# One slot of a chunked recurrence with a feed-forward stage: its small products gathered in three runs

## The chip, the cores and the metric

The kernel runs on one core of a Trainium2 chip. The metric is the device time in microseconds of one execution. TensorE (PE) multiplies matrices, VectorE (DVE), ScalarE (ACT) and GpSimd (POOL) work element by element, and SyncE (SP) issues transfers. [...]

## The reference

For each of 4 x 8 heads a state of 40x40 is carried over 768 positions. Its readings are joined over the heads, and each of the 3072 rows of 320 goes through a feed-forward stage with a gated softmax and a normalization.

```python
for t in range(S):
    y[:, :, t] = np.einsum('bhd,bhde->bhe', rt, state)
    Sa = np.einsum('bhde,bhe->bhd', state, at)
    state_decay = state * wt[:, :, None, :] - np.einsum('bhd,bhe->bhde', Sa, bt)
    state = state_decay + np.einsum('bhd,bhe->bhde', vt, kt)
...
h = x @ w_in
e = np.exp(h - h_max)
sm = e / (np.sum(e, axis=-1, keepdims=True) + 1e-09)
solu = h * sm
ln = (solu - mu) / np.sqrt(var + 1e-06) * g_ln
return (ln @ w_out).astype(np.float32)
```

## The kernel before

The 768 positions are cut into 12 chunks of 64. Two batches with 8 heads each make one item, so 24 items i follow each other, in turn from the two pairs of batches; item i uses the state that item i - 2 left. Within a chunk the recurrence becomes a triangular system, which is solved with the inverse of two 32x32 diagonal blocks and a coupling between them.

The main loop has one turn, called a slot, for each i from -1 to 27. A slot works on several items at once: it answers and reads item i, prepares scores and couplings of item i + 1, keys of items i + 5 to i + 8, and the feed-forward stage of items that were read two to four slots before (m = i - 1, with m - 3, m - 2 and m - 1). TensorE, GpSimd, VectorE and SyncE execute in the order in which the program names the steps; only ScalarE's order is found by the scheduler. So the order of the calls in the loop is the order of the queues.

The steps, by the names that the profile shows:

- `front` transposes a (pa) and b (pb); VectorE forms aT, ScalarE copies bT. `decay` makes the cumulative decays (lw, pcum, ei, inv), `decay_turned` turns them (pei, ex), `scaled` multiplies b and k on GpSimd (kb).
- `norm` multiplies aT and bT (pnt); VectorE masks the product (nt), and a transfer brings it to memory. `begin_inverse` reads it back in blocks (blk) and puts a generator into a list; `some(n)` takes n steps from that list, each of two VectorE operations (prod, uu; L415 and L417). An inverse of 30 steps serves two items; its result goes out (uu_dram) and `bring` fetches it into tu and uh. `narrow` does the same steps, and in the first slots it also converts parts of the weights.
- `flip` transposes a part of tu on VectorE (L442). `couple` multiplies nt with it (py), ScalarE scales the result (wy, L454). `close` multiplies wy with uh (pz), and the copy completes tu.
- `attend_kv` and `attend_rs` transpose k, v, r (pk, pv, pr) and the state (pst). `scores` forms two products (ps); VectorE masks them into psi and lv.
- `carried` and `driven` form the right-hand side (px) out of the state and out of psi; ScalarE copies it to x0. `solved` multiplies with the inverse (pu; nuT, lu). `answered` multiplies with rT (pl), masked into lu.
- `read` forms answers and new state (pyo) in two halves: own (row half and column half of the array equal) and not own. `leave` scales them on VectorE (x, tot) and GpSimd (st) and sends x by transfers to xT; `left` sends the rest of it.
- `hidden` is the first feed-forward product (h): for k-tiles 0 and 1 with 128 rows, for k-tile 2 two products of 64 rows. `exped` takes the maximum (nmax, VectorE) and the exponential (e, ScalarE), `weighed` multiplies e by h, `spreadof` takes the statistics (bs, mv, c; all VectorE), `folded` transposes e (plnT), `output` is the second product (po) in two halves of four.

PSUM has three pools: two buffers of the shape of `banks` (pnt, py, pz, px, ps, pu, pl, pyo in turn), two of `bank` (all transposes, pcum, po), and one h. A product that takes a buffer waits until the readers of the tile two allocations back are done.

The small products are 64x64 (or 40x64): a helper orders 16 of them so that neighbours use different quarters of the array. Where two groups add into the same result from different rows of the array, `fence` puts a drain of TensorE between them. Before, there are two: between `carried` and `driven`, and between the halves of `read`.

Of the kernel before, what the change touches and what calls it, by code (L numbers as in the profile page):

```python
# [17 lines left out]
P = 128  # L18
# [3 lines left out]
GRP = 2  # L22
# [26 lines left out]
def kernel(  # L49
# [204 lines left out]
        nc.tensor.matmul(o, lhsT=lhsT, rhs=rhs, start=start, stop=stop, skip_group_check=True)  # L254


    def fence():
        nc.tensor.drain()

# [19 lines left out]
    def ok(i):  # L279
        return 0 <= i < N  # L280


    def load_keys(i, names, queue=nc.sync):
        if not ok(i):
            return
        for n, ap in (("w", w), ("b", b), ("a", a), ("k", k)):
            if n in names:
                x = a_t[i % 4] if n == "a" else two.tile([P, H, D], FP32, tag="raw_" + n, name="raw_" + n,
                                                             bufs=3)
                st[i]["raw_" + n] = x  # L290
                load(x, ap, i, queue)
# [18 lines left out]
    def decay(i):  # L310
        if not ok(i):
            return
        d = st[i]
        lw = two.tile([P, DM], FP32, tag="lw", name="lw", bufs=1)
        nc.scalar.activation(out=lw, in_=d["raw_w"].rearrange("p h d -> p (h d)"), func=AF.Ln)
        t = (bank("pcum") if i > 5 else ps2.tile([P, DFF], FP32, tag="h", name="h"))[:, 0:DM]
        nc.tensor.matmul(t, lhsT=c_("cum"), rhs=lw, start=True, stop=True)
        nc.scalar.activation(out=ei_t[0][:, :, 0:D], in_=heads(t), func=AF.Exp)
        inv = d["inv"] = two.tile([P, DM], FP32, tag="inv", name="inv", bufs=4)
        nc.scalar.activation(out=inv, in_=t, func=AF.Exp, scale=-1.0)  # L320
# [10 lines left out]
    def turned(name, x):  # L331
        t = bank("p" + name)
        for j in range(4):
            nc.tensor.transpose(out=t[0:W2, j * P:(j + 1) * P],  # L334
                                in_=x[:, 2 * j:2 * j + 2].rearrange("p a b -> p (a b)")[:, 0:W2], identity=ident)
        return t[0:W2].rearrange("p (j b t) -> p b j t", j=4, b=2)
# [4 lines left out]
    def kept(name, t, bufs=1):  # L341
        o = tokens(name, bufs)
        nc.scalar.copy(out=o[0:W2], in_=t)
        return o
# [7 lines left out]
    def front(i):  # L352
        if not ok(i):
            return
        d = st[i]
        t = turned("a", d["raw_a"])
        aT = d["aT"] = tokens("aT", AHEAD)
        nc.vector.tensor_tensor(out=aT[0:W2], in0=t, in1=d["ex"][0:W2, :, :, 0:C], op=ALU.mult)
        d["bT"] = kept("bT", turned("b", d["kb"][:, H:]))

    def masked(dst, t):
# [112 lines left out]
        d["kT"] = kept("kT", turned("k", d["kb"]))  # L474
        d["vT"] = kept("vT", turned("v", v_t[0]))

    def attend_rs(i):
        if not ok(i):
            return
        d = st[i]  # L480
        bp, ci = where_(i)
        d["rT"] = kept("rT", turned("r", r_t[0]), 2)
        if ci:
            t = bank("pst")
            for x in range(4):
                nc.tensor.transpose(out=t[0:W2, x * P:(x + 1) * P],
                                    in_=st_t[bp][:, 2 * x:2 * x + 2].rearrange("p a b -> p (a b)")[:, 0:W2], identity=ident)
            d["s"] = two.tile([P, 4, P], FP32, tag="s", name="s")
            nc.scalar.copy(out=d["s"][0:W2], in_=t[0:W2].rearrange("p (x t) -> p x t", x=4))

    def scores(i):
# [33 lines left out]
    def driven(i):  # L525
        if not ok(i):
            return
        d = st[i]
        if d["opened"]:
            fence()  # L530
        for u in in_turn(lambda p, q, g, h: (p, p ^ h)):
            p, q, g, h = u
            j = 2 * q + g
            mm(d["px"][half(p ^ h), h, j * D:j * D + D], d["psi"][half(p), h, j],
               d["lv"][half(p), head(u), C:W2], start=(h, p ^ h) not in d["opened"])
            d["opened"].add((h, p ^ h))
        nc.scalar.copy(out=x0[:, :, :, 0:D], in_=d["px"][:, :, 0:4 * D].rearrange("p h (j d) -> p h j d", j=4))
# [31 lines left out]
    def read(i, own):  # L569
        if not ok(i):  # L570
            return
        d = st[i]
        bp, ci = where_(i)
        if own:
            d["po"] = banks("pyo")
            d["opened"] = set()
            if ci:
                for u in in_turn(lambda p, q, g, h: (q, h)):
                    p, q, g, h = u
                    at = (2 * p + g) * W2  # L580
                    mm(d["po"][half(h), q, at:at + C], d["s"][rows(q), 2 * p + g, h * C:h * C + C], valued(d["rT"], u),
                       start=(q, h) not in d["opened"], stop=False)
                    d["opened"].add((q, h))
        else:
            fence()
        for g in range(2):
            for j in range(2):
                for u in in_turn(lambda p, q, g, h: (p, h), [u for u in units if (u[0] == u[1]) == own and u[2] == g]):
                    p, q, g_, h = u
                    at = (2 * p + g) * W2  # L590
                    mm(d["po"][half(h), q, at:at + W2], d["kb"][half(p), j * H + head(u)],
                       d["lu" if j else "lv"][half(p), head(u), 0:W2], start=(q, h) not in d["opened"], stop=j == 1)
                    d["opened"].add((q, h))
# [44 lines left out]
    def hidden(i, some):  # L638

        if not ok(i):  # L640
            return
        d = st[i]
        for kt, x in some:
            if (kt, x) == (0, 0):
                d["h"] = ps2.tile([P, DFF], FP32, tag="h", name="h")
            part = slice(0, P) if kt < 2 else half(x)
            mm(d["h"][:, 512 * x:512 * x + 512], d["xT"][part, kt], w_in[part, 2 * kt + (x if kt < 2 else 0)],
               start=kt == 0, stop=kt == NK - 1)

    def exped(i):  # L650
        if not ok(i):
# [61 lines left out]
    def some(n):  # L713
        while steps and n:
            if next(steps[0], steps) is steps:
                steps.pop(0)
            else:
                n -= 1
# [18 lines left out]
    for i in range(4):  # L737
        scaled(i, "b")
        if i == 3:
            scaled(0, "k")  # L740
            scaled(1, "k")
        front(i)
        decay(i + 1)
        norm(i)
        decay_turned(i + 1)
        if i == 0:
            load_keys(2, "ba")
        if i == 1:
            load_keys(3, "w")
            begin_inverse(0)  # L750
            narrow(2)
            load_keys(3, "ba")
            load_keys(0, "k")
            load_keys(4, "w")
            some(8)
        if i == 2:
            load_values(0)
            load_keys(1, "k")
            some(8)
    load_keys(5, "w")  # L760
    load_keys(4, "ba")
    begin_inverse(1)
# [7 lines left out]
    decay(5)  # L770
    load_keys(6, "w")
    land(3, nc.sync)
    some(14)
    load_keys(5, "ba")
    load_values(1)
    bring(0)
# [2 lines left out]
    for n in (4, len(lands)):  # L779
        land(n, nc.sync)  # L780


    shares = {-1: (0, 6, 2, 6), 0: (0, 6, 4, 6), 1: (0, 6, 3, 6), 2: (0, 6, 3, 6), 3: (0, 6, 3, 6)}
    narrowed = {-1: (0, 1), 0: (1, 1), 1: (1, 2), 2: (1, 2), 3: (1, 1)}
    for i in range(-1, N + 3 + LAG):
        j, m = i + AHEAD, i - LAG
        pieces = shares.get(i, (3, 6, 0, 6))
        some_weights = narrowed.get(i, (0, 0))

        some(pieces[0])  # L790
        if i >= 1:
            bring(i + 1)
        if i >= 0:
            load_values(i + 2)
        carried(i)
        driven(i)
        front(j)
        hidden(m - 2, ((0, 1),))
        if i == 3 + LAG:
            centred(mean, 6)  # L800
        load_keys(j + 3, "w")
        load_keys(j + 2, "bak")
        narrow(some_weights[0], pieces[1])

        solved(i)
        attend_kv(i + 1)
        hidden(m - 2, ((1, 1),))
        norm(j)
        attend_rs(i + 1)
        hidden(m - 2, ((2, 0), (2, 1)))  # L810
        exped(m - 2)
        decay_turned(j + 1)
        scaled(j + 1)
        left(i - 1)

        answered(i)
        if i >= 0:
            flip(i + 1)
        weighed(m - 2)
        spreadof(m - 2)  # L820
        decay(j + 2)
        if i == 0:
            turn_g()
        if i == 2 + LAG:
            mean = mean_begun(6)
        output(m - 3, 0)
        if ok(j) and j % GRP == GRP - 1:
            begin_inverse(j // GRP)
        some(pieces[2])
        scores(i + 1)  # L830
        if i < 0:
            flip(i + 1)
        couple(i + 1)
        output(m - 3, 1)
        narrow(some_weights[1], pieces[3])

        close(i + 1)
        read(i, True)
        read(i, False)
        by_value(i + 2)  # L840
        leave(i)
        folded(m - 2)
        hidden(m - 1, ((0, 0), (1, 0)))


# [28 lines left out]
```

## Time and profile before

| | us |
|---|---|
| median of three runs | 640.13 |
| lowest, highest | 639.94, 641.92 |
| the profiled execution | 639.79 |
| its span, first to last instruction | 637.7 |

| stretch of the span | PE busy | DVE busy | clock granted to TensorE |
|---|---|---|---|
| 60 to 110 (first slots) | 35.68 of 50 | 43.81 | 0.70 |
| 110 to 170 | 51.68 of 60 | 53.79 | 0.85 |
| 333.9 to 356.4 (one slot) | 22.28 of 22.5 | 17.61 | 1.00 |
| 356.4 to 378.8 (the next) | 22.18 of 22.4 | 17.34 | 1.00 |

Busy is the time in which an engine executed something; the clock is the share of the full TensorE clock that was granted. In the timelines a line has start, duration, engine, line or operation, what was written and read, the shapes, and in brackets the idle time before and what ended it. [...] the duration of one overlaps the start of the next: step from start to start, or from end to end in the chain of waits.

### The profile page before, as it was taken

What the parts mean: (1) busy time and instruction counts of PE and PEld (TensorE: products, weight loads), DVE (VectorE), ACT (ScalarE), POOL (GpSimd) and SP (SyncE); (2) the same over time, 40 slices, a digit from 0 to 9 for tenths busy, and PEclk for the clock granted to TensorE, in tenths of its full rate; (3) what the DMA queues carried; (4) which work ended last, traced back from release to release, by engine and by line L of the source; (5) the groups of instructions that cost most, each with busy time, mean ns of one, the idle gap of its engine ahead of it and who ended that gap; (6) DMA issues with size and microseconds to landing.
All of it is one profiled execution on the core that took longest, in us unless ns stands there. A gap on an engine that the chain in (4) does not pass through costs nothing.

```text
span 637.7 us, 26729 instructions
## 1 busy us (share of the span) xinstructions
PE 567.5 (89%) x11451; PEld 399.6 (63%) x11451; DVE 461.9 (72%) x1286; ACT 245.3 (38%) x498; POOL 269.1 (42%) x444
## 2 busy tenths in 40 slices
PE   5245677988999999999999999999999999999995
PEld 3134555756577677667667767666776666766653
DVE  4678799999878778778878777787887796443431
ACT  3412545554334434433443443344243333332221
POOL 3334345574274444445543642743544642222200
PEclk9665676688999999999999999999999999999998
DMA  8939896474355535544554553654423422210000
GB/s 166 159 73 169 170 164 131 107 152 87 71 110 93 111 87 95 107 93 103 103 120 79 108 116 73 119 107 95 91 53 70 98 49 49 51 36 26 24 20 21
DMA packets 217868, 59.92 MB, mean 94 GB/s; under 512 B 203216, under 2 KB 213048, under 8 KB 217752
## 3 DMA queue, kind: packets, MB, share of 16 engines
q1 hardware_dynamic: 200984, 34.47, 31.7%
q0 software_dynamic: 11376, 19.25, 12.6%
q10 hardware_dynamic: 5392, 4.51, 2.5%
q8 instruction: 90, 1.47, 1.0%
q14 instruction: 26, 0.21, 0.1%
HBM read 40.10 MB, written 13.37 MB: 84 GB/s over the span
## 4 chain that ended last, share of the span: by engine, by line
PE 71%; DVE 13%; DMA 6%; issue 4%; ACT 2%; SPq 2%; POOL 1%; DVEq 0%; ACTq 0%; POOLq 0%
PE h L254 16%; PE po L703 14%; PE pyo L254 7%; PE px L254 4%; PE pu L254 3%; DVE uu L417 3%; PE plnT L692 3%; PE ps L254 3%; DVE prod L415 3%; PE pl L254 2%; PE pr L334 2%; PE pnt L254 2%; PE pk L334 2%; PE pa L334 2%; PE pz L254 2%
## 5 line engine op out<-in xcount | busy, mean ns | idle before, releaser
L254 PE MATMUL h<-w_in,xT 128*128 128x512 f32 (+1 forms) x288 | 121.6, 614 | 0.0
L415 DVE TENSOR_TENSOR prod<-blk,uu 128x30 f32<-128x30 f32 (+4 forms) x360 | 99.0, 275 | 24.0 <-DMA blk<-nt_dram 14.0
L703 PE MATMUL po<-w,lnT 128*128 128x320 f32 x384 | 113.5, 440 | 0.0
L417 DVE TENSOR_TENSOR uu<-uu,prod 128x30 f32<-128x30 f32 (+4 forms) x360 | 101.9, 283 | 12.4
L703 PEld LDWEIGHTS po<-w,lnT 128*128 128x128 f32 x384 | 70.5, 190 | 29.3 <-issue 2.3
L655 DVE TENSOR_REDUCE nmax<-h 128x1 f32<-128x1024 f32 x24 | 29.4, 1224 | 60.0 <-PE h L254 59.9
L388 POOL DMA_DIRECT2D nt_dram<-nt x20 | 18.3, 916 | 119.0 <-DVE nt L362 97.7
L254 PEld LDWEIGHTS h<-w_in,xT 128*128 128x128 f32 (+1 forms) x288 | 38.9, 190 | 21.9 <-issue 20.8
L623 POOL TENSOR_TENSOR st<-tot,ex 104x160 f32<-104x160 f32 x44 | 22.1, 520 | 70.4 <-DVE tot L619 68.2
L681 POOL TENSOR_TENSOR rs<-c,mhalf 128x1 f32<-128x1 f32 x24 | 13.4, 559 | 91.0 <-DVE c L680 89.6
L635 POOL DMA_DIRECT2D xT<-x x96 | 48.7, 512 | 0.0
L254 PE MATMUL pyo<-lv,kb 64*64 64x104 f32 x768 | 38.6, 274 | 6.0 <-DVE lv L362 3.3
L693 ACT COPY lnT<-plnT 128x512 f32<-128x512 f32 x48 | 26.1, 589 | 43.3 <-PE plnT L692 43.3
L399 POOL DMA_DIRECT2D blk<-nt_dram x42 | 33.3, 800 | 13.0 <-DMA nt_dram<-nt 12.7
L658 ACT ACTIVATE e<-h,nmax 128x1024 f32<-128x1024 f32 x24 | 26.8, 1115 | 28.6 <-DVE nmax L655 27.5
L254 PE MATMUL pyo<-lu,kb 64*64 64x104 f32 x768 | 37.2, 266 | 0.0
L664 DVE TENSOR_TENSOR e<-h,e 128x1024 f32<-128x1024 f32 x24 | 29.4, 1225 | 10.1 <-ACT e L658 10.1
L276 POOL DMA_DIRECT2D raw_r<-in_r_dram x48 | 34.9, 729 | 0.3 <-issue 0.3
L672 DVE BATCH_NORM_STATS2 bs<-e 128x6 f32<-128x512 f32 x48 | 30.9, 686 | 0.8
L707 ACT ACTIVATE osb<-po,rs 128x320 f32<-128x320 f32 x24 | 12.7, 528 | 48.5 <-PE po L703 29.6
L254 PEld LDWEIGHTS pnt<-aT,bT 40*64 40x64 f32 x768 | 14.6, 144 | 26.5 <-issue 25.0
L254 PEld LDWEIGHTS pyo<-lv,kb 64*64 64x64 f32 x768 | 23.9, 145 | 11.3 <-issue 7.7
(130 smaller groups left out, 1127.0 us busy)
## 6 DMA issues: line engine op xcount, KB each, us to landing
blk<-nt_dram POOLq DMA_DIRECT2D x42, 128.0 KB, 4.2
nt_dram<-nt POOLq DMA_DIRECT2D x20, 256.0 KB, 3.5
raw_w<-in_w_dram SPq DMA_DIRECT2D x48, 80.0 KB
a<-in_a_dram SPq DMA_DIRECT2D x48, 80.0 KB
raw_r<-in_r_dram POOLq DMA_DIRECT2D x48, 80.0 KB, 3.3
lv<-in_v_dram SPq DMA_DIRECT2D x48, 80.0 KB
out_dram<-osb ACTq DMA_DIRECT2D x24, 160.0 KB
raw_b<-in_b_dram SPq DMA_DIRECT2D x44, 80.0 KB
```

Source lines behind the costliest of these rows:

```text
L254: nc.tensor.matmul(o, lhsT=lhsT, rhs=rhs, start=start, stop=stop, skip_group_check=True)
L276: queue.dma_start(out=x[half(p), :, 0:D], in_=ap[2 * bp + p, :, ci * C:(ci + 1) * C, :].rearrange("h t d -> t h d"))
L334: nc.tensor.transpose(out=t[0:W2, j * P:(j + 1) * P], in_=x[:, 2 * j:2 * j + 2].rearrange("p a b -> p (a b)")[:, 0:W2], identity=ident)
L399: queue.dma_start(out=nb[home:home + Q], in_=blocks[n][:, Q * e:Q * e + Q, Q * e:Q * e + Q])
L415: nc.vector.tensor_tensor(out=t, in0=nb[:, j:j + 1, j + 1:Q].to_broadcast([P, n_c, m]), in1=u[:, 0:n_c, j:j + 1].to_broadcast([P, n_c, m]) ...
L417: nc.vector.tensor_tensor(out=u[:, 0:n_c, j + 1:Q], in0=u[:, 0:n_c, j + 1:Q], in1=t, op=ALU.subtract)
L635: nc.gpsimd.dma_start(out=xT[to:to + Q, 2], in_=x[at + P - 3 * D:at + D, 2])
L655: nc.vector.tensor_reduce(out=nmax, in_=d["h"], axis=AX.X, op=ALU.max, negate=True)
L658: nc.scalar.activation(out=e, in_=d["h"], func=AF.Exp, bias=nmax, accum_out=d["esum"])
L664: nc.vector.tensor_tensor(out=d["e"], in0=d["h"], in1=d["e"], op=ALU.mult)
L672: nc.vector.bn_stats(out=bs[:, x], in_=d["e"][:, x * 512:x * 512 + 512])
L703: nc.tensor.matmul(d["out"][:, 0:DM], lhsT=d["lnT"][:, f, :], rhs=w2[:, f, :], start=f == 0, stop=f == NF - 1)
```

## The change

The steps stay the same in what they compute; their order in the slot changes, and some are cut in two. `front` loses its b part to `front_b`; `attend_rs` becomes `attend_r` (the transpose of r) and `stated` (that of the state, with one buffer for s instead of two). `hidden` starts its accumulation with k-tile 2 and ends it with k-tile 1.

A slot then has the order: solved, scores of i + 1; stated, front, one h, front_b, decay_turned, one h, exped, decay, output's first half, weighed, spreadof; flip, couple, norm, answered; output's second half; close, the own half of read, carried of i + 1, the two 64-row products of h, one fence, the other half of read, driven of i + 1; then leave, folded, h, keys and values of i + 2, h, and r of i + 2. `carried` and `driven` are now done a slot earlier, for i + 1, and share the drain of `read`. The steps of the inverse are shared out as 3, 5, 3 and 4 instead of 3, 6, 0 and 6. On VectorE, flip thus stands behind weighed and spreadof of its slot. In the slots before the main loop, some steps of the inverse are moved, and keys, values and r of item 0 are prepared there.

```diff
+    def front_b(i):
+        if not ok(i):
+            return
+        d = st[i]
         d["bT"] = kept("bT", turned("b", d["kb"][:, H:]))
...
-    def attend_rs(i):
+    def attend_r(i):
+        if not ok(i):
+            return
+        st[i]["rT"] = kept("rT", turned("r", r_t[0]), 2)
+
+    def stated(i):
...
-            d["s"] = two.tile([P, 4, P], FP32, tag="s", name="s")
+            d["s"] = two.tile([P, 4, P], FP32, tag="s", name="s", bufs=1)
...
     def driven(i):
-        if d["opened"]:
-            fence()
...
     def read(i, own):
-        else:
-            fence()
...
     def hidden(i, some):
         for kt, x in some:
-            if (kt, x) == (0, 0):
+            if (kt, x) == (NK - 1, 0):
                 d["h"] = ps2.tile([P, DFF], FP32, tag="h", name="h")
...
-               start=kt == 0, stop=kt == NK - 1)
+               start=kt == NK - 1, stop=kt == NK - 2)
...
+        front_b(i)
         decay(i + 1)
+        some(4 * (i > 1))
         norm(i)
...
-            some(8)
+            some(4)
...
-    some(14)
+    some(10)
...
+    attend_kv(0)
+    attend_r(0)
...
     for i in range(-1, N + 3 + LAG):
         j, m = i + AHEAD, i - LAG
-        pieces = shares.get(i, (3, 6, 0, 6))
+        pieces = shares.get(i, (3, 5, 3, 4))
         some_weights = narrowed.get(i, (0, 0))
-
-        some(pieces[0])
         if i >= 1:
             bring(i + 1)
         if i >= 0:
             load_values(i + 2)
-        carried(i)
-        driven(i)
+        some(pieces[0])
+
+        solved(i)
+        scores(i + 1)
+        load_keys(j + 3, "w")
+        load_keys(j + 2, "bak")
+
+        stated(i)
         front(j)
         hidden(m - 2, ((0, 1),))
+        narrow(some_weights[0], pieces[1])
+        front_b(j)
+        decay_turned(j + 1)
+        hidden(m - 2, ((1, 1),))
+        exped(m - 2)
+        scaled(j + 1)
+        left(i - 1)
+        by_value(i + 2)
+        decay(j + 2)
         if i == 3 + LAG:
             centred(mean, 6)
-        load_keys(j + 3, "w")
-        load_keys(j + 2, "bak")
-        narrow(some_weights[0], pieces[1])
-
-        solved(i)
-        attend_kv(i + 1)
-        hidden(m - 2, ((1, 1),))
-        norm(j)
-        attend_rs(i + 1)
-        hidden(m - 2, ((2, 0), (2, 1)))
-        exped(m - 2)
-        decay_turned(j + 1)
-        scaled(j + 1)
-        left(i - 1)
-
-        answered(i)
-        if i >= 0:
-            flip(i + 1)
+        output(m - 3, 0)
+        some(pieces[2])
         weighed(m - 2)
         spreadof(m - 2)
-        decay(j + 2)
+
+        flip(i + 1)
+        couple(i + 1)
+        norm(j)
+        answered(i)
+        if ok(j) and j % GRP == GRP - 1:
+            begin_inverse(j // GRP)
         if i == 0:
             turn_g()
         if i == 2 + LAG:
             mean = mean_begun(6)
-        output(m - 3, 0)
-        if ok(j) and j % GRP == GRP - 1:
-            begin_inverse(j // GRP)
-        some(pieces[2])
-        scores(i + 1)
-        if i < 0:
-            flip(i + 1)
-        couple(i + 1)
         output(m - 3, 1)
         narrow(some_weights[1], pieces[3])
 
         close(i + 1)
         read(i, True)
+        carried(i + 1)
+        if ok(m - 1):
+            hidden(m - 1, ((2, 0), (2, 1)))
+        fence()
         read(i, False)
-        by_value(i + 2)
+        driven(i + 1)
         leave(i)
         folded(m - 2)
-        hidden(m - 1, ((0, 0), (1, 0)))
+        hidden(m - 1, ((0, 0),))
+        attend_kv(i + 2)
+        hidden(m - 1, ((1, 0),))
+        attend_r(i + 2)
```

## The prediction

> **What bounds the kernel now.** I read the engine totals first, then the chain of waits, then the timelines of TensorE and VectorE over one slot, then the granted clock in short stretches. The totals:
>
> ```profile
> PE 567.5 (89%) x11451; PEld 399.6 (63%) x11451; DVE 461.9 (72%) x1286; ACT 245.3 (38%) x498; POOL 269.1 (42%) x444
> ```
>
> The chain of waits over one steady slot (start us, us, what) is nearly all TensorE, back to back:
>
> ```profile
> 358.56 1.09 PE ps L254 x64
> 359.65 0.44 PE py L254 x32
> 360.09 2.35 PE po L703 x8
> ...
> 368.05 0.61 PE px L254 x32
> 368.65 0.11 issue
> 368.76 0.68 PE px L254 x32
> ...
> 374.88 0.57 PE pr L334 x4
> 375.46 0.44 PE pst L486 x4
> ```
>
> A slot takes 22.48 us from py to py (404.44 to 426.92), and TensorE is its bound. The reader should see the surcharge at each change of array shape. The same four transposes cost 0.57 right after 64x64 products (pr) and 0.44 after other transposes (pst); a run of 32 of width 64 costs 0.62 when it comes first and 0.47 when it follows one of its kind (ps: 1.09 = 0.62 + 0.47). So an island of 64x64 products costs 0.15 going in and 0.14 coming out (0.20 before po). A drain costs 0.11 idle and 0.22 restart (0.68 against 0.46): 0.33.
>
> VectorE in the same slot is 17.5 us busy of 22.5, in program order. Its timeline (start us, us, operation):
>
> ```profile
> 354.54 1.23 DVE L655 TENSOR_REDUCE nmax<-h 128x1 f32<-128x1024 f32 x1 [1.39 <-PE h L254]
> ...
> 356.35 0.43 DVE L442 STREAM_TRANSPOSE tu<-tu 128x256 f32<-128x256 f32 x1
> 357.04 1.23 DVE L664 TENSOR_TENSOR e<-h,e 128x1024 f32<-128x1024 f32 x1 [0.26 <-ACT e L658]
> 358.30 1.29 DVE L672 BATCH_NORM_STATS2 bs<-e 128x6 f32<-128x512 f32 x2
> ...
> 360.15 0.68 DVE L362 TENSOR_TENSOR psi<-ps,cst 128x512 f32<-128x512 f32 x1
> ```
>
> The place of flip (the L442 transpose) decides the case. It ends at 356.8, before the long softmax work, and py, which reads what it writes, starts only at 359.6: 2.8 us of slack. Where the slack was missing, TensorE waited; so it did for wy, ScalarE's copy of py:
>
> ```profile
> 68.21 1.08 PE L254 MATMUL py<-tu,nt 64*64 64x32 f32 x32 [1.90 <-DVE tu L442]
> ...
> 128.29 0.68 PE L254 MATMUL pz<-uh,wy 64*64 64x32 f32 x32 [0.59 <-ACT wy L454]
> ```
>
> Last, the clock after a pause. In the busy times by stretch (first number PE, then PEld, DVE, ACT, POOL; then granted clock, DMA share, GB/s), a pause in which TensorE is all but idle is followed by 3.2 us at 0.50:
>
> ```profile
> 120.20:121.70 1.50, 0.07 (x6) 0.04 (x1) 1.35 (x5) 1.50 (x4) 1.50 (x3) 1.00 0.16 46
> 121.80:125.00 3.20, 3.20 (x32) 2.56 (x35) 3.03 (x9) 1.82 (x4) 0.25 (x2) 0.50 0.82 138
> 125.30:127.00 1.70, 1.70 (x74) 1.21 (x66) 1.50 (x3) 0.77 (x2) 1.66 (x3) 1.00 0.75 118
> ```
>
> [...] no operation passes another here, so a late VectorE instruction holds TensorE's whole queue. [...] 1.4 us of idleness in a window was enough to lose the clock at 121.7.
>
> **The change, part by part.** *Fewer islands.* Before, a slot has px; pu; pnt; the 64-row pair of h; pl; ps with py; pz with pyo: seven islands and two drains. After, it has pu with ps; py, pnt, pl; pz, pyo, px with the h pair inside at the one drain. Three islands go: 2 x 0.29 + 0.35 = 0.93. The h pair's way out falls on the drain: 0.14. One drain goes: 0.33. That is 1.40 us a slot, 22.5 to 21.1, if nothing waits.
>
> *Flip moves, and a wait appears.* VectorE's order in the new listing is: leave of slot i-1, three steps of the inverse, psi, lv, aT, five steps, nmax, three steps, weighed, spreadof, flip, nt, lu, four steps, leave. Psi cannot start before ps ends, and flip now stands behind all that follows psi. From starts of the trace: psi and lv 1.19 (360.15 to 361.35), aT 0.60, the eight steps 4.65 (the same sizes of step: 2.75 and 1.87 in one slot of a pair, 3.04 and 1.63 in the other), nmax 1.20, weighed 1.26, statistics and scalars 1.86, flip 0.43: 11.2. With 0.07 to start and 0.05 to release, py starts 11.3 us after ps ends. TensorE has for that time only pst 0.58, pa 0.44, h 0.86, pb 0.44, pei 0.44, h 0.86, pcum 0.54, po 2.15: 6.3 us. It stalls for 5.0 in each slot. Behind py in TensorE's queue stand pnt, pl, the second po, and all of run three, so nothing fills the gap; VectorE's own next inputs (pnt, pl, pyo, the next ps) come from that queue, so VectorE idles in turn. The two halves run one after the other.
>
> *TensorE from py to the end of the next ps*, at full clock: py 0.62; the wait for wy 0.60, since pl takes py's buffer (two of that shape) and pnt covers only part; pl 0.63, po 2.35, pz 0.49, pyo 1.21, px 0.46, h pair to the end of the drain 1.22 (0.09 in, 0.43, a last matmul of 0.59, 0.11), pyo 0.77, px 0.58, plnT 0.93, h 0.86, pk and pv 0.88, h 0.86, pr 0.53, pu 0.98, ps 1.17: 15.1. A slot is 11.3 + 15.1 = 26.4 us at full clock.
>
> *The clock.* Five idle microseconds always cost the clock before py comes. [...] Half speed for 5.1 us costs some 2.4 (po 0.535 for 0.267; the small products 0.91 for 0.52), less 0.24 as the wait for wy vanishes at half speed. Bounds: 0 if short windows do not matter, 5.6 if it takes two windows more. I take 2.2: a slot is 28.6.
>
> *Edits I cost at nothing.* The early pk, pv, pr end 1.5 us or more before the products that read them, past their 0.6 us copies on ScalarE. The copies by_value stand earlier on POOL, behind kb and the xT transfers; pv needs them only at the slot's end. Raw loads move on SP within a slot, and lw, moved ahead of e on ScalarE, uses a load issued a slot earlier. One buffer for s serves: pst follows the read of s by 10 us. The inverse keeps 15 steps a slot and two slots a pair. Bring stands at the slot's start as before; its SP transfers get more time, not less. Begin_inverse comes later: on POOL nt_dram (0.9 to issue, 3.5 to land) and then four blk transfers (3.2 and 4.2) end some 13 us after py, when VectorE has just left leave and still has 3 us until ps. Uncovered, each would cost 0.5 us a slot at most, one transpose copy.
>
> **The sum**, against the profiled execution (span 637.7, time 639.79, so 2.1 lie around it; the median of the runs is 640.13). By py of chunk n: py 5 is at 179.60, py 17 at 449.41, py 19 at 492.72, py 21 at 532.30, py 23 at 571.87.
> - py 5 to 17: 12 x 28.6 = 343.2 against 269.8: +73.4.
> - 17 to 19: 57.2 against 43.3: +13.9 (decay and pei end here, in the shadow of the stall).
> - 19 to 21: no aT, 2 x 28.0 against 39.6: +16.4.
> - 21 to 23: no steps; the chain is h, nmax, e, weighed, statistics, flip, 8.5 after ps: 2 x 25.7 against 39.6: +11.8.
> - Start to py 5: VectorE is nearly full already (12 us idle from 60 to 170). Flip of chunk 5 has some 4 us more ahead of it, and the waits for ps and pyo add about 4: +8, between 0 and 16.
> - After py 23: the last slow stretch +2.4, fewer switches -1.4: +1.
> Together +124.5: span 762, time 764.
>
> **The rivals.** (a) *Stall without clock loss*: slots of 26.4, and 25.8 and 23.6 at the end: 47.0 + 9.5 + 12.0 + 7.6, +6 at the start, -1 at the end: +81, 721. [...] Against: from 84 us on, all four pauses of 1.7 us or more before a matmul (3.06, 1.92, 1.70, 2.37) are followed by a 0.50 stretch. (b) *The clock stays down longer*: the windows after py hold 64-wide products, and one such stretch (111.5 to 114.9, with one 0.11 gap) did not restore it; two more windows at 3.2 a slot are +61: 825. (c) *Faster*: flip comes in time and the 1.40 counts: 19 slots x 1.4 and 4 x 1.1 are 31: 609. It decides if VectorE gets from psi to flip in under 6.3 us. The rows say 11.2, and 6.6 even with no steps at all; so only a wrong reading of the queue allows it.
>
> **How the numbers follow.** Main case 0.80 (alone 740 to 790), (a) 0.08, (b) 0.08, (c) 0.04. The time is the main case's. The range, 715 to 800, holds the main case but for its tails, and (a). Below 0.3% (about 2 us) this measurement tells nothing from no change: slower 0.95, within 0.3% 0.01, faster 0.04.
>
> **What would show it.** In the new trace py should be idle some 5 us before it, released by tu (L448); VectorE idle before psi and before x; the clock at 0.50 after each py for 3.4 to 6.8 us; py to py near 28.6; no lone 64x64 islands between transposes. Wrong if py starts right behind po, or if the clock stays 1.00 through the stall.

## The result, and the profile after

The changed kernel takes 805.05 us (median of 4 runs) against 640.04 for the kernel before on the same chip: 1.256 times the time, 95% interval 1.247 to 1.264. The forecast was 764, range 715 to 800. A second measurement of the same kernel gave 803.43 us (800.26 to 804.34), ratio 1.255 (1.250 to 1.260). Its profile is the one shown below, because one of the four executions behind the first median, the profiled one, was disturbed (1125.96 us); the ratio leaves it out.

The engine totals of the changed kernel (busy us, share of the span, instructions):

```profile
PE 606.2 (76%) x11451; PEld 443.3 (55%) x11451; DVE 473.8 (59%) x1286; ACT 250.1 (31%) x498; POOL 266.3 (33%) x444
```

The instruction counts are those of before. The span grew by 164.5 us, TensorE's busy time by 38.7 and VectorE's by 11.9. So most of the loss is waiting, and TensorE's extra busy time is the same work taking longer.

The waits of TensorE over the whole span (engine, product, line, what ended the wait: us in total, times, longest), first three lines:

```profile
PE py L254 <- DVE tu L448: 140.0, 24, 10.6
PE h L318 <- ACT lw L316: 13.8, 2, 7.1
PE ps L254 <- issue: 7.3, 7, 1.3
```

All 24 py wait for tu, the transpose in `flip`. In the profile before it was one, for 1.9 us. The waits of VectorE from 205 to 610 us, where the steady slots lie:

```profile
DVE x L610 <- PE pyo L254: 82.1, 14, 6.8
DVE nt L368 <- PE pnt L254: 28.0, 14, 2.1
DVE psi L368 <- PE ps L254: 14.8, 11, 2.7
```

VectorE waits too, but at other times: for pyo 5.9 us a slot, for pnt 2.0. The two engines work one after the other. VectorE's timeline of one slot, from the scores to the reading of pyo (start, duration, engine, line, operation, in brackets the idle time before):

```profile
405.38 0.69 DVE L368 TENSOR_TENSOR psi<-ps,cst 128x512 f32<-128x512 f32 x1 [0.18 <-PE ps L254]
...
409.80 1.22 DVE L661 TENSOR_REDUCE nmax<-h 128x1 f32<-128x1024 f32 x1
...
412.84 1.22 DVE L670 TENSOR_TENSOR e<-h,e 128x1024 f32<-128x1024 f32 x1
414.09 1.29 DVE L678 BATCH_NORM_STATS2 bs<-e 128x6 f32<-128x512 f32 x2
...
415.95 0.45 DVE L448 STREAM_TRANSPOSE tu<-tu 128x256 f32<-128x256 f32 x1
418.50 0.69 DVE L368 TENSOR_TENSOR nt<-pnt,cst 128x512 f32<-128x512 f32 x1 [2.11 <-PE pnt L254]
...
428.45 0.76 DVE L610 TENSOR_TENSOR x<-pyo,ex 104x256 f32<-104x256 f32 x2 [5.97 <-PE pyo L254]
```

From psi to the end of flip it is 11.02 us without a gap. TensorE in the same slot:

```profile
409.29 2.32 PE L709 MATMUL po<-w,lnT 128*128 128x320 f32 x8
416.45 1.08 PE L254 MATMUL py<-tu,nt 64*64 64x32 f32 x32 [4.85 <-DVE tu L448]
417.32 1.11 PE L254 MATMUL pnt<-aT,bT 40*64 40x64 f32 x32
418.21 1.08 PE L254 MATMUL pl<-rT,nuT 40*64 40x64 f32 x32
419.22 4.63 PE L709 MATMUL po<-w,lnT 128*128 128x320 f32 x8
423.78 0.85 PE L254 MATMUL pz<-uh,wy 64*64 64x32 f32 x32
424.46 0.66 PE L254 MATMUL pyo<-rT,s 40*64 40x64 f32 x32
...
434.84 0.64 PE L496 MATMUL pst<-cst,st 128*104 128x128 f32 x4
```

Set the two po beside each other: 2.32 us ahead of the pause, 4.63 after it. That is the halved clock: 0.50 was granted from 417.45 to 424.20. A product's duration overlaps the next start (py lasts 1.08, and pnt starts 0.87 after it). From py to the first pyo this slot takes 8.01 us, where the rows of before give 4.69 (0.62 + 0.60 + 0.63 + 2.35 + 0.49). From there to pst, at full clock, it takes 10.38, where they give 10.45.

Where the time went, by py of chunks 5, 17, 19, 21 and 23 (us):

| stretch | before | after | more | forecast |
|---|---|---|---|---|
| start to py 5 | 179.60 | 208.39 | 28.8 | 8 |
| py 5 to 17 | 269.81 | 357.28 | 87.5 | 73.4 |
| 17 to 19 | 43.31 | 58.27 | 15.0 | 13.9 |
| 19 to 21 | 39.59 | 57.85 | 18.3 | 16.4 |
| 21 to 23 | 39.57 | 52.67 | 13.1 | 11.8 |
| after py 23 | 65.83 | 67.74 | 1.9 | 1 |
| sum | | | 164.6 | 124.5 |

### The profile page after: what moved, and what is told of

It reads as the page before. It is cut to its first block, busy times and chain, and to the rows that moved or that the text cites. A ratio compares the mean times of both kernels' runs of the same rounds, so it can differ in the third digit from the quotient of the medians.

```text
span 1124.0 us, 26639 instructions
## 1 busy us (share of the span) xinstructions
PE 1017.9 (91%) x11451; PEld 642.5 (57%) x11451; DVE 483.8 (43%) x1286; ACT 253.7 (23%) x498; POOL 265.0 (24%) x444
## 4 chain that ended last, share of the span: by engine, by line
PE 81%; DVE 13%; ACT 3%; issue 2%; DMA 1%; SPq 0%; ACTq 0%; POOL 0%; DVEq 0%
PE h L254 20%; PE po L709 12%; PE pyo L254 9%; PE pu L254 4%; PE ps L254 4%; PE plnT L698 4%; PE px L254 3%; DVE bs L678 2%; PE py L254 2%; DVE e L670 2%; PE pk L335 2%; PE pnt L254 2%; DVE prod L421 2%; PE pst L496 2%; PE pl L254 2%; PE pv L335 2%
## 5 line engine op out<-in xcount | busy, mean ns | idle before, releaser
L254 PE MATMUL h<-w_in,xT 128*128 128x512 f32 (+1 forms) x288 | 245.9, 1160 | 0.0
L709 PE MATMUL po<-w,lnT 128*128 128x320 f32 x384 | 233.0, 801 | 1.7 <-DVE w L233 1.7
L709 PEld LDWEIGHTS po<-w,lnT 128*128 128x128 f32 x384 | 111.3, 295 | 104.1 <-issue 99.7
L610 DVE TENSOR_TENSOR x<-pyo,ex 104x256 f32<-104x256 f32 x48 | 18.1, 419 | 214.7 <-PE pyo L254 204.3
L254 PE MATMUL py<-tu,nt 64*64 64x32 f32 x768 | 25.1, 270 | 61.5 <-DVE tu L448 61.5
L254 PEld LDWEIGHTS h<-w_in,xT 128*128 128x128 f32 (+1 forms) x288 | 64.0, 303 | 25.5 <-issue 21.2
L254 PEld LDWEIGHTS py<-tu,nt 64*64 64x64 f32 x768 | 22.6, 218 | 86.3 <-DVE tu L448 75.0
L254 PE MATMUL pyo<-lu,kb 64*64 64x104 f32 x768 | 61.3, 392 | 0.0
L254 PE MATMUL pyo<-lv,kb 64*64 64x104 f32 x768 | 58.6, 396 | 2.4
L698 PE MATMUL plnT<-cst,e 128*128 128x128 f32 x192 | 46.5, 434 | 0.4 <-PE po L709 0.2
L405 POOL DMA_DIRECT2D blk<-nt_dram x42 | 33.3, 799 | 37.5 <-DMA nt_dram<-nt 36.8
```

The costliest lines, as they stand in the source:

```text
L405: queue.dma_start(out=nb[home:home + Q], in_=blocks[n][:, Q * e:Q * e + Q, Q * e:Q * e + Q])
L698: nc.tensor.transpose(out=t[:, j * P:(j + 1) * P], in_=d["e"][:, f * P:(f + 1) * P], identity=ident)
L709: nc.tensor.matmul(d["out"][:, 0:DM], lhsT=d["lnT"][:, f, :], rhs=w2[:, f, :], start=f == 0, stop=f == NF - 1)
```

## The experiments

**The changed kernel once more** (no edit).

> The changed kernel unchanged, for a profile at the usual clock. Theory A (flip behind the softmax steps stalls py, and the pause costs the clock): py idle about 5 us before each start, released by tu; about 800 us; py to py near 30, because the clock stays at 0.50 for some 9 us a slot and not 5. Rival B (the stall is there, but what slows the slot beyond 26.4 us is something else than the clock, a further wait): py to py near 30 with a clock of 1.00 for most of the slot and a second idle time on TensorE of 2 us or more.

803.43 us. This is the profile shown above. Theory A held: the pause is there, and apart from it TensorE's longest wait from py 5 on is 1.3 us, where rival B needed 2.

**Only flip late, in the kernel before.** If the place of flip is the cause, it must do its harm without any other part of the change.

```diff
         answered(i)
-        if i >= 0:
-            flip(i + 1)
         weighed(m - 2)
...
         scores(i + 1)
-        if i < 0:
-            flip(i + 1)
+        flip(i + 1)
         couple(i + 1)
```

> The kernel before, with nothing changed but flip, which moves behind the softmax steps and the masks of ps, just ahead of py. Theory A (what costs is flip's place, in any order of the slot): py waits 2.3 us a slot, 23 slots, 693 us if the clock holds; and since 2.3 idle us in a window of 3.4 us lose the clock in most slots, some 2 to 3 us more in those, 720 to 760. Rival C (the loss belongs to the three runs): below 660 with a clock as before.

728.29 us (724.30 to 728.94), ratio 1.137 (1.133 to 1.141): one moved instruction costs 88 us. In its timeline py waits in each slot:

```profile
425.23 0.67 PE L254 MATMUL py<-tu,nt 64*64 64x32 f32 x32 [2.28 <-DVE prod L415]
```

The releaser named here (prod) is a neighbour of flip in VectorE's queue. The slots come in two lengths: 25.0 us, which is 22.48 plus the pause and 0.24 more, and 26.6 to 26.7, where one stretch of 3.41 us at clock 0.50 is added. The same 2.28 us of idleness thus lose the clock in some slots and not in others, and such a stretch costs about 1.65 us. The trace shows why. The granted clock changes only at times on one grid of 3.41 us: all 29 changes from 180 us to the end of the span lie within 0.01 us of it. Cut along this grid, the windows from py 5 to py 17 that kept the clock have at most 1.65 us of idleness, and those that lost it 1.76 to 2.28. These are the two nearest to each other (stretch, length, then PE, PEld, DVE, ACT, POOL busy, granted clock, DMA share, GB/s); the second is followed by 3.41 us at 0.50:

```profile
266.93:270.34 3.41, 1.76 (x36) 1.46 (x37) 3.20 (x10) 0.47 (x1) 1.36 (x3) 1.00 0.00 0
475.15:478.56 3.41, 1.65 (x36) 1.40 (x37) 3.20 (x11) 0.47 (x1) 1.36 (x3) 1.00 0.01 2
```

So it matters here how much of a pause falls into one window.

**Flip early, in the changed kernel.** Only `flip(i + 1)` is moved, to right behind `front(j)`.

```diff
         front(j)
+        flip(i + 1)
         hidden(m - 2, ((0, 1),))
...
-        flip(i + 1)
         couple(i + 1)
```

> Only flip is moved, ahead of the five steps of the inverse, behind aT. Theory A: py no longer waits; but nt and lu stand behind spreadof, and pz needs nt's buffer, so a stall of about 1.5 us moves to pz; slots 22.5 to 23, clock 1.00, 640 to 655 us. Rival C (the half clock comes from the three long runs of 64x64 products[...]): the clock stays low in part of each slot, 720 us or more.

732.18 us (726.64 to 738.20), ratio 1.142 (1.135 to 1.148). It wins back 71 us, less than expected. From py 4 on py waits no more than 0.2 us, but in the profiled execution, of 738.20 us, pz waits for VectorE's nt (46.4 us, 17 times over the span, about half of it ahead of py 5), and pl for ScalarE's wy (13.9 us, 11 times). nt comes out of pnt, which the change put behind py, and it still stood behind weighed and the statistics on VectorE. The pauses are shorter but still cost the clock in about half of the slots (0.88 granted on average). So a second wait stood one place behind the first, in the same queue.

**Flip and the masks early.** In addition weighed and spreadof go behind `answered`, so that nt and lu come ahead of them.

```diff
-        weighed(m - 2)
-        spreadof(m - 2)
-        flip(i + 1)
         couple(i + 1)
         norm(j)
         answered(i)
+        weighed(m - 2)
+        spreadof(m - 2)
```

> Flip early as in e2_flip_early, and weighed and spreadof behind answered, so that VectorE masks pnt and pl first. Theory A: no stall but about 0.25 us at pl for wy; slots 21.2 to 21.5, 610 to 620 us, faster than both. If the 1.40 us of switches and drain were not real: slots 22.5, 635 to 640. Rival C: 720 or more.

676.58 us (673.61 to 678.94), ratio 1.057 (1.052 to 1.062). With two moves on VectorE 127 us are back of the 164 that the change cost here. TensorE's waits from 205 to 610 us are now small:

```profile
PE pl L254 <- ACT wy L460: 12.5, 12, 2.1
PE ps L254 <- issue: 7.2, 5, 2.1
PE pei L335 <- DVE aT L359: 4.0, 5, 1.1
```

From py 5 to py 17 the slots take 23.4 us on average, more than before; the shortest takes 21.52. More than half of what is left sits in the first slots: py 5 comes at 200.82, against 179.60 before. There flip now stands ahead of the landing of what it transposes, and VectorE waits for uu_dram 15.9 us, four times, between 66 and 201 us. But 10.3 of these lie ahead of py 0, which comes at 68.26 (68.21 before). Between py 0 and py 5 TensorE's pz waits 19.2 us for nt; what makes nt late there was not traced.

**Three more moves** on top of that: exped, scaled and the steps of the inverse behind `answered`, other shares, and flip later again in the first slots.

```diff
-        pieces = shares.get(i, (3, 5, 3, 4))
+        pieces = shares.get(i, (6, 5, 2, 2))
...
-        exped(m - 2)
-        scaled(j + 1)
...
         answered(i)
+        scaled(j + 1)
+        exped(m - 2)
+        some(pieces[2])
         weighed(m - 2)
```

> A try at a version that beats both: e3_flip_and_masks_early, with nmax and e behind py, pnt and pl so that ScalarE copies wy first, with kb's products on GpSimd behind the transfer of nt, six steps of the inverse at the slot's start (6, 5, 2, 2), and in slots 0 to 3 flip behind the conversions and three steps at the start. Theory A with 1.40 us a slot saved: slots 21.3 to 22, py 5 at 185 to 200, 620 to 645 us. If e3's remaining loss has another source (the rest of the queue's order): 665 to 680, as e3.

681.69 us (680.54 to 689.86), ratio 1.068 (1.062 to 1.075): no gain over the two moves. With six steps of the inverse ahead of psi, VectorE waits for the landing of blk (36.8 us in all) and psi gets late; py 5 is at 200.55 as before.

**Filling the pause.** Ahead of py, in slots 5 to 22, stand eight more products 128x320 whose result is not used. They take nothing away from the wait for flip; they only keep TensorE busy.

```diff
+        if 4 < i < N - 1:
+            t = bank("pfill")
+            for c in range(8):
+                nc.tensor.matmul(t[:, 0:DM], lhsT=c_("mean"), rhs=w2[:, c, :], start=c == 0, stop=c == 7)
         couple(i + 1)
```

> The changed kernel with eight products of the mean's matrix with w2 (128x320, 4.3 us at full clock, result unused) put ahead of py in slots 5 to 22; nothing else is changed, flip stays late. It does more work. Theory A with the clock as the second half of the cost: TensorE is idle for less than 1 us, keeps its clock, slots 26.5, 720 to 735 us, faster than the changed kernel although it does more. Rival B: 800 or more.

771.21 us (769.41 to 772.50), ratio 1.205 (1.200 to 1.211): 32 us less than the changed kernel, with more work in it. The busy times by stretch (columns as above) around a py at 406.08:

```profile
401.80:405.20 3.40, 3.31 (x13) 2.01 (x11) 2.91 (x6) 0.64 (x2) 0.00 (x0) 1.00 0.52 87
405.20:408.60 3.40, 2.41 (x98) 2.07 (x99) 1.94 (x7) 0.47 (x1) 0.85 (x2) 1.00 0.02 3
408.60:412.00 3.40, 3.40 (x103) 2.63 (x101) 2.39 (x9) 0.90 (x2) 0.65 (x1) 1.00 0.35 82
```

About 1 us of idleness is left, and the clock stays. Every second slot is then 26.56 to 26.63 us, beside the 26.4 that the forecast gives at full clock; the others take 28 to 29.8; in five slots pei waits for aT, 8.0 us in all, and the rest of their excess was not traced. The changed kernel's mean slot from py 5 to 17 is 29.77, some 3.2 us more. Of these 2.7 lie between py and the first pyo, where it has the low clock (7.42 us on average, 4.73 here): this is what the clock costs. The forecast of 720 to 735 was missed for those longer slots and for the first slots, which were not filled (py 5 at 208.40).

**Filling it with small products.** The same, with 144 products 64x64x32 (result not used) instead of the eight large ones.

```diff
+            t = banks("pfill")
+            for c in range(9):
+                for u in in_turn(lambda p, q, g, h: (p ^ h, p)):
+                    p, q, g, h = u
+                    x = half(p ^ h)
+                    mm(t[half(p), h, (2 * q + g) * Q:(2 * q + g) * Q + Q], st[i + 1]["nt"][x, h, 2 * q + g],
+                       w2[x, c % NF, 0:Q])
```

> As e4_filled_stall, but the 4 us ahead of py are filled with 144 products of 64x64 with 32 columns, of py's own shape, on two banks, result unused. It tells what the clock's windows count. If small products count as work like large ones: as e4, slots 26.5 to 28.5, about 770 us. If they count too little (theory for the low stretches that lasted a window more when py, pnt and pl fell in it): the clock is lost in every slot as in the changed kernel, slots 29 or more, 795 to 815 us.

830.75 us (823.97 to 835.68), ratio 1.295 (1.289 to 1.301). The clock was lost in nearly every slot (0.50 in 15 of the 16 between py 6 and py 22). But the string of small products has pauses of its own, of 1 to 2 us, which the profile puts down to "issue" (18.0 us, 15 times, before pfill between 205 and 650 us). The pauses alone do not explain it. Cut along the grid of 3.41 us, nine windows with 1.28 to 1.38 us of idleness and 123 to 128 small products lost the clock here (one with 1.31 kept it), while six windows of the large filling with 1.5 to 1.8 us of idleness and 6 to 10 large products kept it. So beside small products a shorter pause lost the clock here.

**One drain, in the kernel before.** What are the savings worth where no wait covers them? Flip and the masks stay where they were; only px of item i + 1 moves to the drain of the answers, and its own drain goes.

```diff
-        carried(i)
-        driven(i)
         front(j)
...
         read(i, True)
+        carried(i + 1)
+        fence()
         read(i, False)
+        driven(i + 1)
```

> The kernel before with one part of the change alone: the right-hand side (px) of item i + 1 is formed at the end of the slot, around the drain of the answers (pyo), so that px's own island and one drain are gone; flip, masks and all other steps stay where they were. If the saving was real and only the place of flip spoiled it, a slot loses 0.29 (island) and 0.33 (drain) = 0.62 us, and 23 slots 14 us: 626 us. Rival: the savings are not there, since x0 or VectorE's reading of pyo is late at the new place: 640 or more, with TensorE waits for pu or px.

634.46 us (631.28 to 635.78), ratio 0.991 (0.988 to 0.993). A steady slot is 21.85 us, 0.63 less than 22.48; 0.62 was worked out. The total gains less than the slots, since two of them are about 1 us longer by a pause named "issue", and the first slots are some 2 us later.

**And the pair of h at the drain.**

```diff
-        hidden(m - 2, ((2, 0), (2, 1)))
...
         carried(i + 1)
+        if ok(m - 1):
+            hidden(m - 1, ((2, 0), (2, 1)))
         fence()
```

`hidden` starts with k-tile 2, as in the change.

> The same, and the 64-row pair of h moved to the drain, as the change has it. If its island (0.29) goes and 0.09 comes back at its entry, 0.20 x 23 = 4.6 us less than with px alone: 621 us. Rival: its transfers of x, which the pair of k-tile 2 now needs almost a slot earlier, come too late at the drain, and the answers behind it wait: above 626.

632.82 us (632.59 to 634.18), ratio 0.990 (0.987 to 0.992). The steady slot went up, to 22.14. TensorE's timeline has the reason, where the pair had stood between pst and pei:

```profile
396.24 0.65 PE L334 MATMUL pr<-cst,r 128*104 128x128 f32 x4
396.72 0.60 PE L486 MATMUL pst<-cst,st 128*104 128x128 f32 x4
397.56 0.65 PE L334 MATMUL pei<-cst,ei 128*104 128x128 f32 x4 [0.24 <-ACT rT L343]
```

Pei takes pr's buffer, so it waits until ScalarE has copied rT. The pair had covered that copy; a plain step from one transpose to the next is 0.44, here it is 0.84.

**Another product of h over the copy.** K-tile 1 of h moves to the place that the pair left.

```diff
-        hidden(m - 2, ((1, 1),))
         norm(j)
         attend_rs(i + 1)
+        hidden(m - 2, ((1, 1),))
```

> The version with one drain and the h pair at it, with one product of h (k-tile 1) moved from ahead of pnt to behind the transpose of the state, where the pair of h had stood. With the pair gone from there, pei waits 0.24 us for ScalarE's copy of rT in each slot, 0.40 us from pst to pei more than a plain transpose's step. If that uncovered copy is what ate the pair's gain, the wait is gone and 0.3 to 0.4 us a slot, 7 to 9 us, are won: 624 to 626 us. Rival: pr then follows pk and pv after pnt alone (0.6 us) and waits for ScalarE's copy of kT instead, the wait only moves: 630 to 635.

630.25 us (628.74 to 631.84), ratio 0.986 (0.984 to 0.988). The wait is gone, and the steady slot is 21.76:

```profile
413.38 0.62 PE L486 MATMUL pst<-cst,st 128*104 128x128 f32 x4
413.84 1.02 PE L254 MATMUL h<-w_in,xT 128*128 128x512 f32 x2
414.70 0.60 PE L334 MATMUL pei<-cst,ei 128*104 128x128 f32 x4
```

In the last slots, which have no pnt, pr now waits for the copy of kT instead:

```profile
557.74 0.62 PE L334 MATMUL pr<-cst,r 128*104 128x128 f32 x4 [0.60 <-ACT kT L343]
```

**Each place where it is needed.** The product stands behind pst only in slots that still have pnt.

```diff
+        if not ok(j):
+            hidden(m - 2, ((1, 1),))
         norm(j)
         attend_rs(i + 1)
-        hidden(m - 2, ((1, 1),))
+        if ok(j):
+            hidden(m - 2, ((1, 1),))
```

> The version with the product of h behind the transpose of the state, but only in slots that still have pnt; in the last slots, which have neither pnt nor pei, the product stands ahead of pr again. In the last four slots the version with h behind pst everywhere steps by 19.96 us (pr waits 0.6 us for the copy of kT), the one with h ahead of pr by 19.12. If each place is right for its slots, 4 to 5 slots x 0.84 = 3 to 4 us are won: 626 to 627. Rival: what stands between is set by other things in the last slots, or the pauses that the profile shows as issue take it back: 629 to 631.

627.17 us (626.49 to 629.93), ratio 0.980 (0.978 to 0.981). This version beats both kernels, with two parts of the change that touch no order on VectorE and one product of h put over a copy.

**Pl with the scores.** One island more was taken away from the version with the pair at the drain, by moving `answered` to just ahead of `scores`.

```diff
-        answered(i)
         if i >= 0:
             flip(i + 1)
...
+        answered(i)
         scores(i + 1)
```

> The same, and the product pl moved behind the second-stage products, directly ahead of the scores ps, so that it has no island of its own. If islands are all there is, 0.29 x 23 = 6.7 us less: 614 us. Rival: py, which takes pl's buffer, waits for VectorE's mask of pl, which now comes after weighed and the statistics[...], and a wait of more than 0.3 us a slot eats the gain: 621 or more.

670.37 us (668.73 to 675.02), ratio 1.049 (1.045 to 1.052). The rival held. The two lines of the timelines, TensorE's and VectorE's:

```profile
424.45 0.67 PE L254 MATMUL py<-tu,nt 64*64 64x32 f32 x32 [0.95 <-DVE lu L362]
```

```profile
423.71 0.68 DVE L362 TENSOR_TENSOR lu<-pl,cst 128x512 f32<-128x512 f32 x1
```

Py takes pl's buffer, and the mask lu, which empties it, comes on VectorE behind the statistics. Most slots are 23.42 to 23.46 us, about 1.29 more than without the move; the wait shown is 0.95 of that, and the rest was not traced. It is the fault of the change in small: a product moved on TensorE, and its reader on VectorE not looked at.

## Why the prediction was wrong

The direction, the mechanism and most steps were right; the sum was 40 us short (164.6 against 124.5), and the time lay 5 us above the range. Three terms failed. The largest is "Start to py 5: +8": it measured 28.8, half of the miss. The clock, "I take 2.2" a slot, measured 2.7, some 6 us up to py 17. And pauses of ps that the profile names "issue" have no term in the sum: they lengthen seven slots from py 5 on by some 10 us together.

*Fewer islands, one drain.* Right, as far as it could be seen. The part of a slot from the first pyo to pst measured 10.38 at full clock against 10.45 worked out. In the run with two moves, the slot from py 16 to 17, in which TensorE waits for nothing, takes 21.52 us; the rows give 21.4 (15.1 and 6.3, the wait for wy among them). And px's part alone, in the kernel before, gave 0.63 a slot against 0.62. The pair's part (0.20) is not seen clean: together with px and the covered copy the slot lost 0.72.

*Flip moves, and a wait appears.* Right. 11.2 us from psi to flip's end were expected, 11.02 measured; a stall of 5.0, and 4.7 to 5.2 from chunk 6 to 17. From the end of ps to py it is 11.37 us in the slot shown (434.84 to 446.21), against 11.3. The run with flip alone moved shows the cause by itself. What the prediction did not see is that nt stands in the same line: with flip early, pz waits for it.

*The clock.* That the stall costs the clock held (0.50 after all 18 of them from chunk 6 on, of 4.1 to 6.3 us); the size was short. The term said 3.4 to 6.8 us of low clock after py, 5.1 on average, and 2.2 us a slot. In chunks 6 to 17 the low stretch after py is 4.7 to 7.9 us, about 6.4 on average. The way from py to the first pyo is 7.42 us on average from py 5 to 17, 2.7 more than the 4.69 of the rows (3.3 more in the slot shown, one of the dearest). That is 0.5 us a slot above the term. As much again, 0.57 us a slot, lies between the first pyo and pst: not the clock, but five slots in which ps waits 0.7 to 1.3 us for "issue". Two more such slots make up 3.2 of the 4.3 us that the stretches from py 17 to 23 are short. The term took it that the clock comes back with the first window, one step of the grid of 3.41 us, in which TensorE is busy throughout; this was the author's estimate, and it is the step that failed. In the profile before, 0.50 lasted one such step from 121.7, from 131.9 and from 155.9, with TensorE idle for at most 0.11 us in it. Here are six stretches of the changed kernel, each inside one window, in which TensorE was busy throughout (columns as above). The first three start 2.0 to 4.5 us after py, and the clock returned at the end of their window; the last three start 0.5 to 1.0 us after py, and it did not:

```profile
478.90:482.20 3.30, 3.30 (x28) 1.85 (x28) 1.29 (x5) 0.46 (x1) 0.13 (x1) 0.50 0.34 79
448.20:451.50 3.30, 3.30 (x37) 2.40 (x33) 2.83 (x10) 0.00 (x0) 0.95 (x1) 0.50 0.23 53
420.90:424.20 3.30, 3.30 (x22) 1.77 (x24) 1.44 (x5) 0.31 (x1) 0.00 (x0) 0.50 0.34 79
417.45:420.75 3.30, 3.30 (x71) 2.79 (x68) 2.02 (x5) 0.47 (x1) 0.95 (x1) 0.50 0.02 5
475.50:478.80 3.30, 3.30 (x64) 2.62 (x56) 2.18 (x6) 0.46 (x1) 0.72 (x1) 0.50 0.02 5
506.20:509.50 3.30, 3.30 (x81) 2.79 (x75) 1.83 (x5) 0.47 (x1) 0.95 (x1) 0.50 0.02 5
```

The counts beside PE tell them apart: 22 to 37 products in the windows that restored it, mostly of po; 64 to 81 in the others, mostly py, pnt and pl. In seven of the twelve slots from py 5 on such a window came first. So rival (b), with its chance of 0.08, named a true cause and took it too large: it set two windows more for every slot, where it was one more in a part of them. Another reading would be that the windows that failed start too soon after the pause. Two further windows speak against it. The first, of the kernel with flip alone moved, starts 0.7 us after py, holds products of po, and restored the clock. The second, of the changed kernel, starts 4.1 us after py, behind a window that was busy too, and did not:

```profile
294.30:297.60 3.30, 3.30 (x7) 2.13 (x8) 2.40 (x9) 0.47 (x1) 2.19 (x4) 0.50 0.59 142
147.80:151.10 3.30, 3.30 (x94) 3.22 (x88) 3.09 (x12) 1.66 (x4) 0.23 (x1) 0.50 0.34 79
```

Cut along the grid, thirteen traces of this case (before, the changed kernel and the eleven variants) hold 166 windows at 0.50 in which TensorE was busy for over 98.5% of the time. All 84 in which fewer than 40 products start restored the clock; of the 27 with more than 75, two did. So one window that the profile shows busy does not always bring the clock back: 25 of these 27 did not. Whether the number of products counts, or the small part of the array that each uses, is not told apart.

*Start to py 5, "+8, between 0 and 16".* This is half of the miss: 28.8, outside its own bounds. The step gave flip 4 us more ahead of it and 4 for the waits for ps and pyo, because VectorE is nearly full there. From py 0 to py 5 VectorE's busy time grew by 5.6 us, near the first 4; its idle time grew by 22.5. There it waits for ps 11.3 us, for pnt 10.5 and for pyo 3.3, and before it waited for none of them. The wait for pnt, from flip through py and pnt to nt, was not in the sum at all. Nor was the clock, which the sum prices only from py 5 on: TensorE was at half clock for 82 us between py 0 and py 5, against 40 before, and for 10 to 12 us after each of py 0 to 3. In the new trace, VectorE and TensorE in the slot that ends with py 4:

```profile
160.32 0.69 DVE L368 TENSOR_TENSOR psi<-ps,cst 128x512 f32<-128x512 f32 x1 [4.61 <-PE ps L254]
...
174.53 0.45 DVE L448 STREAM_TRANSPOSE tu<-tu 128x256 f32<-128x256 f32 x1
```

```profile
163.69 0.70 PE L318 MATMUL pcum<-lw,cst 128*128 128x320 f32 x2
175.03 1.08 PE L254 MATMUL py<-tu,nt 64*64 64x32 f32 x32 [10.64 <-DVE tu L448]
```

The line from psi to flip is 14.7 us here, since the conversion of weights and the start of the inverse lie in it too, and TensorE has no po to fill it (no item has come so far). Its first five py wait 46.2 us. A full VectorE was taken as a cushion: it meant that the strict order would cost more, as each wait of VectorE for TensorE is then lost for good. How the 28.8 us divide between waits and clock was not tried apart. The runs with flip early bring little of py 5 back (200.8 in the run with two moves, where pz waits for nt); how much of the head the moved steps of the inverse cost by themselves was not tried.

*Edits at nothing.* No wait for pk, pv, pr, the state copy or the raw loads became large: besides py, TensorE's waits from 205 to 610 us come to 5 us. The cover that was missed stands in another run: the pair of h covers ScalarE's copy of rT in the order of before (0.40 us a slot).

*Stretches after py 17.* The terms were 13.9, 16.4 and 11.8; measured 15.0, 18.3 and 13.1, most of the difference in two slots with the pause of ps (19 and 21). The pauses are 6.0 to 6.3 us before py 19 to 21, and 4.09 before the last two.

## What to carry to other kernels

Before gathering work on the bounding engine, write down for every moved product who reads it and who makes its input, and follow those in their own queues: here the 0.62 us of px's island and drain were to be had in each slot, but one 0.43 us transpose behind the softmax on VectorE cost 88 us by itself. Make such a change in parts: the part that left VectorE's order alone, with one product put over a copy, gave 2% less time, the whole 26% more. A pause is priced with what may follow it at half clock (here 1.65 us after eight of thirteen pauses of 2.28 us), and a piece of work that seems moved for free may have been the cover of a copy.

## What the runs showed that was not expected

Filling a pause with useless large products made the kernel faster, 803 to 771 us, because it kept the clock (0.91 on average, against 0.83). From py 5 to py 23 the low stretches are whole multiples of 3.41 us: mostly one in the kernel before with flip alone moved (11 of 14, the others two), two or three in the changed kernel.

In these runs long strings of small products have pauses for which the profile names no engine. In the changed kernel ps, which follows pu without a change of shape, waits seven times for "issue", up to 1.3 us; with 144 more small products in a slot these pauses reach 2.0 us. In the version with one drain, two steady slots had one of 0.8 to 0.9 us, in pyo and px.

Late steps of the inverse on VectorE take some 0.28 us alone and up to 1.19 while GpSimd works beside them. In the slot shown above, of the changed kernel:

```profile
431.82 1.19 DVE L421 TENSOR_TENSOR prod<-blk,uu 128x117 f32<-128x117 f32 x1
```

```profile
431.98 0.88 POOL L330 TENSOR_TENSOR kb<-raw_b,inv 128x320 f32<-128x320 f32 x1
```

This step and the next (0.82 us) lie beside the two kb products, and take 0.5 to 0.9 us more than such a step alone. The step before them took 0.97 us, mostly beside transfers that GpSimd issues, so kb is not the whole of it. What makes the steps longer was not shown.
